# The first batch of a retention block by chunks of 128 tokens in half-array products, with other load and step orders

## Chip, cores and metric

One core of a Trainium2 chip runs the whole program. The metric is the device time of one execution in microseconds (us); lower is better. The kernel before takes 1019.66 us (median of 3 runs, 1018.57 to 1022.64).

## The reference

Retention (attention with a decay in place of the softmax) over 8 batches, 8 heads, 576 tokens and a head width of 64, then a feed-forward block over the 4608 x 512 result, all in float32:

```
scores = scale * q @ k^T                            # per batch and head, 576 x 576
Dmat   = gamma[h] ** (i - j) where i >= j, else 0
ret    = (scores * Dmat) @ v
x      = ret as (8*576) x (8*64)                    # the bridge
g      = x @ w_gate                                 # 512 x 1536
out    = (g * sigmoid(g) * (x @ w_val)) @ w_out     # 1536 x 512
```

The q, k and v are float32; the three weights come as float64.

## The kernel before

**Tiling.** Two heads make a pair, one in partitions 0 to 63, the other in 64 to 127, so a batch has four pairs (HP = 4). Pairs are numbered through all batches: 0 to 3 are the first batch, 4 is the second batch's first. The sequence is cut into chunks of L = 64 tokens; the first batch takes its first 512 tokens here (CW = 512, eight chunks) and its last 64 later, by `end_scores` and its kin. A chunk's output is the product of its own masked scores with v ("own values") plus the product of q with a running state of all earlier chunks ("earlier values").

**One pair of the first batch.** Loads of q, k, v (two heads each, 128 KB apiece). For pairs 1 to 3, q comes in another layout into `early[i]`, and GpSimd (POOL) scales it by the decay into place (`scale_run`, line 735). TensorE (PE) transposes k and q into PSUM banks (line 466); ScalarE (ACT) or VectorE (DVE) copies them to `kT` and `qT` (lines 470 to 473). k is scaled by its decay (`keys`, lines 505 and 507). Then TensorE makes the scores of the eight chunks (line 573, 64x64 products in `inner`), and each chunk's k^T v (`new_states`, line 543). DVE masks the scores with `near` (line 580) and combines the k^T v sums into states (lines 596 to 608). TensorE makes own values (line 532) and earlier values (line 559) in `outer`; DVE or ACT puts them into `xs[0]` (lines 645, 640). A float32 product is two matmul records in the trace.

**The feed-forward's first tile** is the 512 tokens of the first batch. `up0(f, chunks)` makes the hidden block f of 12: for gate and for val, four products over c = 0 to 3 (one per pair) into a bank, 128x512 each (line 853; for some f in halves, line 850). f = 0 uses bankA and bankB, f = 1 bankC and bankE. With c = 3 done, ACT takes the Silu of the gate (line 856) and DVE multiplies with val (line 857).

**Weights** are float64 in HBM and are made float32 in the kernel: `load_w(m)` loads the raw bits (`order` gives which), `split(j)` on ACT makes two parts of a half j (lines 389 and 390), `rounding(j)` on DVE joins them (lines 406 and 407) and then calls `split(j + 1)`. Halves 0 and 1 are gate and val of f = 0, 2 and 3 those of f = 1, 4 and 5 the gate of f = 2 and 3. A raw place is loaded anew once its splits are done; `held` keeps one such load for later. m < 5 goes by SyncE's queue (SP), the rest by ACT's.

**Order.** Behind `tc.manual_schedule` the order on every engine is the program's own; each engine takes its instructions in turn. Before that point a scheduler orders the first loads and selects. The first batch runs in `tick(t, 0, HP)` for t = 0 to 5, in the branch `hi == HP`: pair t is transposed, t - 1 gets scores and states, t - 2 its values. Pairs alternate between two sets of buffers (`places`). At t = 4 and 5 the first up steps stand between: up0(0, c = 0, 1), up0(1, c = 0, 1), then c = 2 and 3. `tick(HP, HP, FIRST)` begins the second batch, with up0(2) next.

Of the kernel before, what the change touches and what calls it, by code (L numbers as in the profile page):

```python
# [22 lines left out]
def tables(gamma, scale, L):  # L23
# [13 lines left out]
    runs = scale * (g[None, :, None] ** ((4 * lane[:, :, None] + np.arange(4)) % L)).reshape(2 * L, -1)  # L37
    parts = [twice((g[:, None] ** -at).T), twice((g[:, None] ** (L - at)).T),
             both(g[:, None] ** L), both(g[:, None] ** (2 * L)), pieces, runs, both(scale * g[:, None] ** at),
# [92 lines left out]
def kernel(  # L132
# [121 lines left out]
    def load(i):  # L254
# [6 lines left out]
        if i < HP:  # L261
# [4 lines left out]
            for h, queue in zip(heads, queues):  # L266
                if scaled(i):
                    queue.dma_start(out=early[i][:, ts(h % 2, CW // 2)], in_=q[b, h, 0:CW].rearrange("(p c) d -> p (c d)", c=NFULL))
                else:
                    queue.dma_start(out=blocks(qk)[:, h % 2], in_=q[b, h, 0:CW].rearrange("(c p) d -> p c d", p=P))  # L270
            for h, queue in zip(heads, queues):
                queue.dma_start(out=blocks(kn)[:, h % 2], in_=k[b, h, 0:CW].rearrange("(c p) d -> p c d", p=P))
            for h in heads:
                queues[i % 2].dma_start(out=blocks(t)[:, h % 2], in_=v[b, h, 0:CW].rearrange("(c p) d -> p c d", p=P))
# [21 lines left out]
    def chunk(i, hl, c):  # L296

        if whole(i):
            g, r = divmod(NC * hl + c, 2)
            return half[r], slice(g * D, (g + 1) * D)  # L300
        if c + 1 == NC:
            return half[hl], slice(CW, CW + D)
# [7 lines left out]
    NCOL = 6 * H + 4 * HP  # L310
    nc.sync.dma_start(out=tab[:, 0:NCOL], in_=decays[:, 0:NCOL])
    load(0)
    load(1)
    ident = const.tile([P, P], F32, name="ident")
    make_identity(nc, ident)
    nc.scalar.activation(out=io[:, 0:1], in_=ident[:, 0:1], func=AF.Silu)
    inv, key = tab[:, 0:H], tab[:, H : 2 * H]
    step = tab[:, 2 * H : 2 * H + 2 * HP]
    piece = tab[:, 2 * H + 2 * HP : 2 * H + 4 * HP]
    run = tab[:, 2 * H + 4 * HP : NCOL]  # L320
# [12 lines left out]
    for rows in half:  # L333
        decay(slice(0, H), slice(0, H), rows)

    load(2)
    nc.sync.dma_start(out=tab[:, NCOL:], in_=decays[:, NCOL:])
    load(3)
# [72 lines left out]
    for f in range(2):  # L411
        for m in range(2):
            load_w(m, (f,))
    load_w(2)
    load_w(3)

# [4 lines left out]
    other = (spare[:, 0:CW].rearrange("p (h c i) -> p h c i", h=2, i=L), None,  # L421
             spare[:, CW : CW + NC * D].rearrange("p (c d) -> p c d", d=D))
# [5 lines left out]
    for t in (state, other[2]):  # L428
        nc.gpsimd.memset(t[:, 0], 0.0)

    def places(i):
        return other if i < HP and i % 2 else (ret, ret_last, state)

# [10 lines left out]
    def vector(i):  # L444

        return i == 0

    def transposes(i):
        p = i % HP
        qk, kn, vt = loaded.pop(i)  # L450
        qT = early[i] if i < HP else qp.tile([P, S], F32, tag="qT", name="qT")
# [3 lines left out]
        copy = nc.scalar.copy if i else nc.vector.tensor_copy  # L455
        if i < HP:

            mine = (bankC, bankE) if i + 1 == HP else (bankB, bankA)
            parts = [(kT, kn, mine[0]), (qT, qk, mine[1])]
            if i == 0:  # L460
                parts.reverse()

            def turn(t, src, bank):
                for c in range(NFULL):
                    to = bank[:, c : 4 * P : NFULL] if t is qT and scaled(i) else bank[:, ts(c, P)]
                    nc.tensor.transpose(to, src[:, ts(c, P)], ident)

            def put(t, _, bank):
                if i or t is qT:
                    copy(t[:, 0:CW], bank)  # L470
                else:
                    copy(t[:, 0 : CW // 2], bank[:, 0 : CW // 2])
                    nc.scalar.copy(t[:, CW // 2 : CW], bank[:, CW // 2 :])

            if i + 1 == HP:
                for part in parts:
                    turn(*part)
                pieces = [lambda part=part: put(*part) for part in parts]
# [1087 lines left out]
```

## Time and profile before

| What | us |
|---|---|
| median of 3 runs | 1019.66 |
| profiled execution | 1019.5 |
| its span, first to last instruction | 1017.8 |
| PE busy / DVE busy / ACT busy / POOL busy in the span | 1001.0 / 715.5 / 286.4 / 555.2 |
| PE's longest wait in the first 260 us: for the first q | 4.5 |
| the next: in front of line 532, behind line 389 on ACT | 2.0 |
| the next: line 864's bankE for DVE's line 857, at 125.6 | 1.1 |

Span and busy times are of the profiled execution. Engines work side by side, so a busy share says little by itself; what counts is which engine waits for which at which place. PE is busy for 98% of the span, so time is to be had where PE waits. "L466" is line 466. In a row of the timeline, `x32` counts the records, the bracket gives the engine's idle time before and what ended it, and a matmul's end is modelled: the next one may begin before it. The first profiled instruction starts at 0.

### The profile page before, as it was taken

To read this page: it belongs to the slowest core of one execution; us is meant where nothing else is said; L and a number is where in the kernel's file an instruction comes from. 1 tells how busy PE (TensorE), PEld (TensorE's weight loads), DVE (VectorE), ACT (ScalarE), POOL (GpSimd) and SP (SyncE) were. 2 spreads that over 40 slices of the span, in tenths; PEclk is the share of its full clock that TensorE was granted. 3 is DMA by queue.
4 is the path that set the end of the run, shared out by engine and by line. 5 is a ranking of instruction groups with operands and counts; after the bars stand their busy time and mean duration, and the time that the engine had idled before them with its cause. 6 is when DMAs were issued, how large, how long until landed. Compare 5 with 4: busy or idle time off the path is not lost.

```text
span 1017.8 us, 21317 instructions
## 1 busy us (share of the span) xinstructions
PE 1001.0 (98%) x8336; PEld 823.8 (81%) x8336; DVE 715.5 (70%) x1215; ACT 286.4 (28%) x636; POOL 555.2 (55%) x579
## 2 busy tenths in 40 slices
PE   6999999999999999999999999999999999999998
PEld 4654455888888888888888888888888888888887
DVE  5478887678787765967778678866575767566644
ACT  4465622122423312133322102233320012232110
POOL 3400349979472218575565247756672586566615
PEclk9999999999999999999999999999999999999999
DMA  9999977867586887657677777434454554445552
GB/s 243 256 258 246 222 223 251 253 202 198 136 248 166 248 216 209 189 172 195 177 210 204 184 183 207 166 125 167 163 174 141 150 192 145 148 159 174 186 160 94
DMA packets 278892, 194.38 MB, mean 191 GB/s; under 512 B 212552, under 2 KB 246088, under 8 KB 278792
## 3 DMA queue, kind: packets, MB, share of 16 engines
q1 hardware_dynamic: 251464, 94.70, 36.5%
q10 hardware_dynamic: 26688, 97.92, 29.1%
q8 instruction: 66, 1.08, 0.4%
q0 software_dynamic: 640, 0.39, 0.2%
q14 instruction: 34, 0.28, 0.1%
HBM read 154.04 MB, written 38.93 MB: 190 GB/s over the span
## 4 chain that ended last, share of the span: by engine, by line
PE 85%; DMA 6%; DVE 4%; ACT 2%; POOL 2%; issue 1%; SPq 0%; ACTq 0%; DVEq 0%; POOLq 0%
PE bankB L1186 11%; PE bankC L1186 11%; PE bankA L1186 11%; PE bankE L1186 11%; PE bankB L1381 7%; PE bankC L1381 7%; PE bankE L1381 6%; PE bankA L1381 6%; PE outer L1186 2%; PE inner L1186 2%; DMA kn<-in_k_dram 2%; PE outer L532 2%; PE outer L559 1%; DMA rest<-in_moe_w_val_dram 1%; PE inner L573 1%
## 5 line engine op out<-in xcount | busy, mean ns | idle before, releaser
L1042 POOL TENSOR_TENSOR rest<-rest 128x512 f32<-128x512 f32 (+1 forms) x141 | 150.3, 1077 | 162.5 <-DVE rest L1042 114.2
L1201 POOL TENSOR_TENSOR arena<-rest,io 128x256 f32<-128x256 f32 x156 | 115.0, 749 | 75.9 <-ACT io L1200 75.3
L1200 ACT ACTIVATE io<-rest 128x256 f32<-128x256 f32 x192 | 79.3, 417 | 205.1 <-DVE rest L1042 140.8
L1186 PE MATMUL bankB<-rest,arena 128*128 128x256 f32 x448 | 114.6, 380 | 0.2 <-DVE rest L1042 0.2
L1186 PE MATMUL bankC<-rest,arena 128*128 128x256 f32 x416 | 106.5, 381 | 0.0
L1042 DVE TENSOR_TENSOR rest<-bankB,rest 128x512 f32<-128x512 f32 x116 | 78.4, 684 | 39.7 <-PE bankB L1186 26.4
L1186 PE MATMUL bankA<-rest,arena 128*128 128x256 f32 x412 | 104.7, 379 | 0.0
L1042 DVE TENSOR_TENSOR rest<-bankA,rest 128x512 f32<-128x512 f32 x110 | 74.4, 684 | 38.8 <-PE bankA L1186 19.3
L1042 DVE TENSOR_TENSOR rest<-bankC,rest 128x512 f32<-128x512 f32 x110 | 74.5, 684 | 38.7 <-PE bankC L1186 25.6
L1042 DVE TENSOR_TENSOR rest<-bankE,rest 128x512 f32<-128x512 f32 x106 | 71.6, 683 | 35.5 <-PE bankE L1186 17.0
L1186 PE MATMUL bankE<-rest,arena 128*128 128x256 f32 x372 | 95.2, 381 | 0.7 <-DVE rest L1042 0.7
L1186 PEld LDWEIGHTS bankB<-rest,arena 128*128 128x128 f32 x448 | 84.7, 190 | 12.2 <-DVE rest L1042 0.6
L1186 PEld LDWEIGHTS bankC<-rest,arena 128*128 128x128 f32 x416 | 78.4, 190 | 11.9 <-DVE rest L1042 1.2
L1186 PEld LDWEIGHTS bankA<-rest,arena 128*128 128x128 f32 x412 | 78.2, 190 | 10.7
L1186 PEld LDWEIGHTS bankE<-rest,arena 128*128 128x128 f32 x372 | 70.0, 190 | 11.8 <-DVE rest L1042 1.6
L1042 POOL TENSOR_TENSOR arena<-arena 128x256 f32<-128x256 f32 (+1 forms) x76 | 70.6, 953 | 10.5 <-DMA up<-arena 6.0
L886 POOL TENSOR_TENSOR rest<-rest 128x512 f32<-128x512 f32 x21 | 28.5, 1377 | 74.7 <-DVE rest L407 59.4
L1381 PE MATMUL bankB<-arena 128*128 128x256 f32 x264 | 61.0, 381 | 0.0
L1381 PE MATMUL bankE<-arena 128*128 128x256 f32 x264 | 60.8, 380 | 0.0
L886 POOL TENSOR_TENSOR arena<-arena 128x768 f32<-128x768 f32 x24 | 47.0, 1961 | 16.0 <-DVE arena L1201 15.4
L1381 PEld LDWEIGHTS bankE<-arena 128*128 128x128 f32 x264 | 50.0, 190 | 6.8
L1381 PEld LDWEIGHTS bankB<-arena 128*128 128x128 f32 x264 | 49.8, 190 | 6.9
(267 smaller groups left out, 1886.7 us busy)
## 6 DMA issues: line engine op xcount, KB each, us to landing
arena<-up ACTq DMA_DIRECT2D x63, 896.0 KB, 4.6
arena<-dn ACTq DMA_DIRECT2D x65, 384.0 KB, 3.0
arena<-dn SPq DMA_DIRECT2D x39, 384.0 KB, 3.2
out_dram<-rest SPq DMA_DIRECT2D x31, 256.0 KB, 3.2
qk<-in_q_dram SPq DMA_DIRECT2D x108, 72.0 KB, 4.3
qk<-in_k_dram SPq DMA_DIRECT2D x108, 72.0 KB, 3.0
dn<-rest SPq DMA_DIRECT2D x26, 256.0 KB, 2.7
up<-arena SPq DMA_DIRECT2D x13, 512.0 KB, 6.4
```

What stands on the lines that cost most here:

```text
L532: m = nc.tensor.matmul(value(i, hl, c), s["v"][rows, at], ret[rows, c % 2 if whole(i) else hl, c // 2], start=start, stop=start, skip_grou ...
L559: nc.tensor.matmul(xr[half[hl]] if c + 1 == NC else value(i, hl, c), state[half[hl], c, :], s["qT"][half[hl], ts(c, L)], start=False, stop ...
L573: nc.tensor.matmul(sc[chunk(i, hl, 2 * c + r)[0], r if whole(i) else hl, c], kT[half[hl], at], qT[half[hl], at], start=True, stop=True, sk ...
L886: eng.tensor_tensor(out=dst, in0=srcs[0], in1=srcs[1], op=ALU.add if op[0] == "add" else ALU.subtract)
L1042: eng.tensor_tensor(out=out, in0=a, in1=b, op=ALU.add if sign > 0 else ALU.subtract)
L1186: m = nc.tensor.matmul(b[:, g * TB : (g + 1) * TB], w[:, g], x, start=(opens and g == 0), stop=True, skip_group_check=True)
L1200: nc.scalar.activation(out=s, in_=src[:, 0:TB], func=AF.Silu)
L1201: (nc.vector if busy and o != 2 else nc.gpsimd).tensor_tensor(out=hid[:, qd, 2 * H + h, 2 * T + t], in0=src[:, TB : 2 * TB], in1=s, op=ALU ...
L1381: nc.tensor.matmul(b[:, m * TB : (m + 1) * TB], lhs[:, qd, ts(m, P)], w[:, qd], start=(opens and qd == 0 and m == 0), stop=(qd == NQ - 1), ...
```

## The change

Of the first batch's four pairs, and of the loads around them, it changes this:

- The first batch leaves `tick` and gets functions of its own (`first_turn`, `first_put`, `first_scores`, `first_masks`, `first_sums`, `first_states`, `first_values`, `first_out`). A chunk has 128 tokens: four chunks instead of eight. Scores are 64 rows by 128 columns of the array, 128 columns moving, 8 products per pair instead of 16; sums are 128 rows by 64 columns, 8 instead of 16; own values 128 rows by 64 columns with 128 columns moving, 8 instead of 16; earlier values 6 instead of 14.
- A mask of its own, `first_near` (128 x 8 x 128, one select of 1024 columns on POOL) in place of the first two selects of `near`, which are now made later. The masked scores are 1024 columns per pair instead of 512. Three state steps per pair instead of five DVE steps. The output of a pair is one instruction of 512 columns.
- All four pairs use the same buffers: `inner` for scores, one half of `outer` for values and the other for sums, one set for masked scores; all transposes go through bankC and bankE.
- Loads: the first table grows from 64 to 208 columns and goes behind the first q half; pair 1's q and k go ahead of the v of pairs 0 and 1; the first half of the first gate block goes ahead of pair 3, and the rest of the tables behind all first weights. Pair 4's load is called first of all in the hand-written part.
- The order: up0(0) gate, c = 0 to 2, stands ahead of the fourth pair's scores, up0(0) val ahead of its values, and up0(1) follows; `rounding(1)` stands behind the fourth pair's states, `rounding(3)` behind the steps with c = 3 of up0(0); the held load and `split(4)` stand behind up0(1).

The core of the diff; first tables and loads:

```
-    runs = scale * (g[None, :, None] ** ((4 * lane[:, :, None] + np.arange(4)) % L)).reshape(2 * L, -1)
+    runs = scale * (g[None, :, None] ** ((4 * lane[:, :, None] + np.arange(4)) % (2 * L))).reshape(2 * L, -1)
...
+                if i == 0 and queue is nc.sync:
+                    nc.sync.dma_start(out=tab[:, 0:NCOL], in_=decays[:, 0:NCOL])
...
-            for h in heads:
-                queues[i % 2].dma_start(out=blocks(t)[:, h % 2], in_=v[b, h, 0:CW].rearrange("(c p) d -> p c d", p=P))
+
+            def values():
+                for h in heads:
+                    queues[i % 2].dma_start(out=blocks(t)[:, h % 2], in_=v[b, h, 0:CW].rearrange("(c p) d -> p c d", p=P))
+
+            loaded[i] = (qk, kn, t)
+            return values
...
-    NCOL = 6 * H + 4 * HP
-    nc.sync.dma_start(out=tab[:, 0:NCOL], in_=decays[:, 0:NCOL])
-    load(0)
-    load(1)
+    NCOL = 8 * H + 4 * HP + P
+    values = [load(0), load(1)]
     ident = const.tile([P, P], F32, name="ident")
     make_identity(nc, ident)
     nc.scalar.activation(out=io[:, 0:1], in_=ident[:, 0:1], func=AF.Silu)
+    for f in values:
+        f()
+    load(2)()
...
-    for rows in half:
-        decay(slice(0, H), slice(0, H), rows)
-
-    load(2)
-    nc.sync.dma_start(out=tab[:, NCOL:], in_=decays[:, NCOL:])
-    load(3)
+    first_near = arena[:, 2048:3072].rearrange("p (h i) -> p h i", i=P)
+    first_ret = arena[:, 1024:2048].rearrange("p (h c i) -> p h c i", h=2, i=P)
+    nc.gpsimd.affine_select(out=first_near, in_=first_inv.unsqueeze(2).to_broadcast([P, H, P]), compare_op=ALU.is_ge, fill=0.0,
+                            base=0, channel_multiplier=-1, pattern=[[0, H], [1, P]])
...
-    for f in range(2):
-        for m in range(2):
-            load_w(m, (f,))
+    load_w(0, (0,))
+    load(3)()
+    load_w(1, (0,))
+    for m in range(2):
+        load_w(m, (1,))
     load_w(2)
     load_w(3)
+    nc.sync.dma_start(out=tab[:, NCOL:], in_=decays[:, NCOL:])
```

The pair's new functions:

```
+    def first_scores(i):
+        for c, hl in first:
+            nc.tensor.matmul(inner[:, hl, ts(c, P)], kT[half[hl], ts(c, P)], st[i]["qT"][half[hl], ts(c, P)],
+                             start=True, stop=True, skip_group_check=True)
+
+    def first_masks(i):
+        for hl in range(2):
+            nc.vector.tensor_tensor(out=first_ret[:, hl], in0=inner[:, hl].rearrange("p (c i) -> p c i", i=P),
+                                    in1=first_near[:, 2 * i + hl].unsqueeze(1).to_broadcast([P, NFULL, P]), op=ALU.mult)
+
+    def first_sums(i):
+        s = st[i]
+        for c, hl in first:
+            nc.tensor.matmul(sums[half[hl], c], s["kn"][:, head(c, hl)], s["v"][:, head(c, hl)],
+                             start=True, stop=True, skip_group_check=True)
+
+    def first_states(i):
+        (nc.scalar.copy if i else nc.vector.tensor_copy)(out=even[:, 0], in_=sums[:, 0])
+        for c in range(1, NFULL):
+            nc.vector.scalar_tensor_tensor(out=even[:, c] if c + 1 < NFULL else end_states[:, i], in0=even[:, c - 1],
+                                           scalar=step[:, HP + i : HP + i + 1], in1=sums[:, c], op0=ALU.mult, op1=ALU.add)
+
+    def first_values(i):
+        s = st.pop(i)
+        for c, hl in first:
+            own = nc.tensor.matmul(outer[half[hl], 0, ts(c, P)], s["v"][:, head(c, hl)], first_ret[:, hl, c],
+                                   start=(c == 0), stop=(c == 0), skip_group_check=True)
+        wait = nc.tensor.nop()
...
+        for c, hl in first[2:]:
+            nc.tensor.matmul(outer[half[hl], 0, ts(c, P)], even[half[hl], c - 1], s["qT"][half[hl], ts(c, P)],
+                             start=False, stop=True, skip_group_check=True)
+
+    def first_out(i):
+        if i:
+            nc.scalar.copy(out=xs[0][:, i], in_=outer[:, 0])
...
```

`first_turn` makes the eight transposes of a pair, `first_put` its copies and the scaling of k. The order by hand, with pairs 2 and 3 in full:

```
-    for t in range(HP + 2):
-        tick(t, 0, HP)
-
-        if t == 3:
-            load(HP)
-        for j in {3: (1,), 5: (4, 5)}.get(t, ()):
-            rounding(j)
-    for c in range(2, HP):
-        for f in range(2):
-            up0(f, [c])
+    early_chunks = range(HP - 1)
+    load(HP)
+    scale_run(1)
+    first_turn(0)
+    first_put(0)
+    first_scores(0)
+    scale_run(2)
+    first_turn(1)
+    first_masks(0)
+    first_put(1)
+    first_sums(0)
+    first_states(0)
+    first_values(0)
+    first_out(0)
+    first_scores(1)
...
+    first_scores(2)
+    first_masks(2)
+    first_sums(2)
+    first_states(2)
+    split(0)
+    first_values(2)
+    first_out(2)
+    first_turn(3)
+    first_put(3)
+    rounding(0)
+    up0(0, early_chunks, (0,))
+    first_scores(3)
+    first_masks(3)
+    first_sums(3)
+    first_states(3)
+    rounding(1)
+    up0(0, early_chunks, (1,))
+    first_values(3)
+    first_out(3)
+    rounding(2)
+    up0(1, early_chunks, (0,))
+    up0(0, [HP - 1])
+    rounding(3, False)
+    up0(1, early_chunks, (1,))
+    up0(1, [HP - 1])
+    while held:
+        held.pop()()
+    split(4)
+    for j in (4, 5):
+        rounding(j)
     load(HP + 1)
+    decay(slice(0, H), slice(0, H), half[0])
```

## The prediction

> **What bounds the kernel now.** First the page: how much of the span TensorE (PE) works, and in which slices it doesn't.
>
> ```profile
> span 1017.8 us, 21317 instructions
> PE 1001.0 (98%) x8336; PEld 823.8 (81%) x8336; DVE 715.5 (70%) x1215; ACT 286.4 (28%) x636; POOL 555.2 (55%) x579
> ...
> PE   6999999999999999999999999999999999999998
> ```
>
> TensorE idles 16.8 us in all, and the one poor slice is the first (25.4 us each). Next the windows of 10 us, to place it. The columns are busy time and number of instructions of PE, PEld, DVE, ACT, POOL, then clock, DMA share and GB/s.
>
> ```profile
> 0.00:10.00 10.00, 4.44 (x74) 3.51 (x75) 1.64 (x4) 2.23 (x4) 3.21 (x11) 1.00 0.96 202
> 10.00:20.00 10.00, 8.06 (x265) 6.67 (x264) 7.66 (x17) 3.80 (x9) 3.90 (x4) 1.00 1.14 262
> 20.00:30.00 10.00, 7.80 (x146) 4.88 (x143) 6.18 (x13) 8.07 (x17) 1.95 (x2) 1.00 1.02 288
> 30.00:40.00 10.00, 9.82 (x81) 4.71 (x80) 4.70 (x11) 5.32 (x10) 6.78 (x13) 1.00 0.99 229
> 40.00:50.00 10.00, 10.00 (x44) 8.15 (x43) 4.72 (x8) 2.68 (x5) 5.71 (x11) 1.00 1.19 275
> ```
>
> The idle time is 5.56 + 1.94 + 2.20 + 0.18 = 9.9 us before 40 us; from 40 to 260 us the same view loses 1.3, of which 1.14 lies at 120 to 130. So a change of this stage can give at most 9.9, and TensorE's lateness at 41 us is passed on nearly whole. Last the timeline of the stage (start, duration).
>
> ```profile
> 9.72 1.11 PE L466 MATMUL bankB<-ident,kn 128*128 128x128 f32 x4 [0.15 <-DMA kn<-in_k_dram]
> 14.30 0.66 PE L466 MATMUL bankB<-ident,rest 128*128 128x128 f32 x4
> 18.90 0.69 DVE L580 TENSOR_TENSOR ret<-inner,near 128x512 f32<-128x512 f32 x1 [0.35 <-ACT even L584]
> 20.12 1.13 ACT L640 COPY rest<-outer 128x256 f32<-128x256 f32 x3 [1.25 <-PE outer L559]
> 23.51 0.59 ACT L470 COPY kT<-bankC 128x512 f32<-128x512 f32 x1
> 24.60 1.98 PE L853 MATMUL bankA<-rest,arena 128*128 128x512 f32 x4
> 25.18 0.43 DVE L406 TENSOR_SCALAR arena<-rest 128x512 int32<-128x512 int32 x1 [0.72 <-ACT rest L389]
> 25.75 0.69 DVE L407 CUSTOM_DVE_ANT_0 arena<-arena,rest 128x1024 uint16<-128x1024 uint16 x1
> 28.23 0.69 PE L573 MATMUL inner<-rest,kT 64*64 64x64 f32 x32
> 28.75 0.65 PE L543 MATMUL inner<-v,rest 64*64 64x64 f32 x32
> 29.33 1.98 PE L853 MATMUL bankC<-rest,arena 128*128 128x512 f32 x4
> 30.98 1.10 DVE L603 SCALAR_TENSOR_TENSOR rest<-rest,tab 128x64 f32<-128x64 f32 x3
> 35.58 0.66 ACT L389 ACTIVATE rest<-rest 128x512 f32<-128x512 f32 x1
> 36.26 1.02 PE L853 MATMUL bankC<-rest,arena 128*128 128x512 f32 x2
> 37.12 1.02 PE L853 MATMUL bankE<-rest,arena 128*128 128x512 f32 x2
> 39.04 0.60 ACT L856 ACTIVATE io<-bankA 128x512 f32<-128x512 f32 x1 [0.47 <-PE bankA L853]
> ```
>
> From these come the prices. An up step (one c, one bank) is 0.86 (36.26 to 37.12). A full-array f32 record costs 0.43 for 512 columns, so 0.11 for 128; a product is two records. Thirty-two 64x64 records take 0.52 (28.23 to 28.75), four side by side. DVE needs 0.69 for a product on 128x512 from PSUM, 1.10 for three dependent 128x64 steps, 0.43 + 0.69 for one rounding. ACT needs 0.59 for a 128x512 copy and, by the rows of line 390 that follow line 389 by 0.57, 1.24 for one split. Before, up steps begin at 24.60 and up0(2) (line 850) at 41.41: 16.81, nearly without a gap.
>
> **The front: pairs 0 to 2.** Per pair TensorE does 16 score records, 16 for own values and 12 for earlier ones at 128 columns and 16 sums at 64, two side by side: 8 x 0.11 + 8 x 0.11 + 6 x 0.11 + 8 x 0.06 = 2.9, against 32 + 32 + 32 + 28 records at some 0.52 each, 2.1, before. No row shows half-array products; the ends are 2.1 (as the quadrants) and 5.7 (52 records one after another at 0.11 or 0.06, or each pair behind a 0.19 weight load). I take 2.9, since the nearest row, the quadrants, runs neighbours at once.
>
> The Trainium skill, TensorEngine Tiling (Array Packing), Key Properties, says that a change of tiling mode drains the array, and this change makes four or five per pair. The trace here shows less: line 853 begins at 29.33, before the modelled end of line 543 at 29.40. A drain of 0.2 at each would add an estimated 1.0 in the fourth pair.
>
> But the order in which a pair's steps follow each other decides, not their sum: scores 0.9 + 0.2 until the last has ended; masks 2 x 0.69 = 1.4 (one before: twice as many columns); states 1.1 on DVE behind the masks (own values lie under this); earlier values 0.65 + 0.2; hand-overs 0.15. That is 4.4 per pair, since the next pair's scores stand behind the earlier values. Pair 0's scores start at 7.8 (line 573 now: 7.58; the wider first table, 104 KB instead of 32, puts 0.3 ahead of k at 250 GB/s), at half rate as line 466 at 9.72 (1.11 against 0.66), so 9.8; its earlier values end at 14.3 because pair 1's transposes and its own sums come between. Pair 1 ends at 19.0, pair 2 at 23.4, the fourth pair's transposes (1.0) at 24.2. So the first up step starts at 24.2 instead of 24.60: -0.4, with -2.5 (products as the quadrants, a shorter pair 0) and +2.5 (0.8 more per pair) as ends.
>
> What goes at nothing: the new mask table on POOL (1024 columns; two selects of 512 took 1.37) is ready at 6.5 and needed at 9.8; the old masks are next used at 60.6. k of pair 1 comes about 1.8 earlier, since v is put behind; but the pair's transposes wait for pair 0's scores at 9.6 anyway. The w_gate half that rounding(0) needs comes at some 15 instead of 19.45, and isn't awaited. Fewer ACT and DVE instructions (1.13 to 0.59 per output, two state steps fewer) are in the 4.4.
>
> **The three waits behind it.** From 24.2 TensorE has the same work as before: 16 up steps x 0.86 = 13.76 and the fourth pair's 2.9 + 0.2, 16.8. But its order, and DVE's, are fixed by hand:
>
> - bankB's first three steps need rounding(1), which on DVE stands behind masks(3) and states(3). These begin when scores(3) end: 0.25 tail + 1.4 + 1.1 + 1.12 + 0.1 = 4.0, less the sums (0.5) that TensorE does meanwhile: 3.5 idle. Before, this rounding ended at 24.5.
> - bankE's steps need rounding(3), now behind the first product of line 857, which needs bankB's last step: 0.3 + 0.69 + 1.12 = 2.1 idle.
> - up0(2) needs rounding(4), and so split(4), which ACT now does after both Silus: from the end of bankE's last step 0.2 + 0.69 + 0.43 + 0.69 + 0.05 = 2.1 on DVE (ACT's side, Silu 0.6 and split 1.24 from bankC's end 0.86 earlier, takes 1.2). Idle 2.1.
>
> Together 7.7. Late next: the load of the third val weights on ACT's queue goes out after these Silus, near 46 instead of 29.60, and its gate after split(5), near 49 instead of 36.85; ACT's Silu and split queue stand behind them. They are needed by up0(4) at about 67 (60.13 now); a load like these took 6.05 (36.85 to 42.90) and 9.21, so 10 us of cover are left. On SP the big table (256 KB, 1 us) now stands ahead of pair 4's q, needed by transposes at 43.35 now, later after. ACT's load itself waits for a q load of pair 5 that SP issues behind the m=4 weights; I put its landing at 45.5 +- 1, so 0 to 1.5 more; I take 0.
>
> **The sum.** -0.4 + 7.7 = +7.3 at up0(2): 48.7 instead of 41.41. Of this 1.1 comes back, the wait of bankE L864 for DVE at 125.6, whose chain runs through loads that are no later (bounds 0 and 1.1). +6.2 on the profiled execution's 1019.5 (span 1017.8 and 1.7 around it; 0.16 under the median shown, 1019.66): **1025.7**. The ends: start -2.5 to +2.5, the ACT wait +1.5, the return 0 to 1.1; its own range is 1023.5 to 1028.5.
>
> **Rivals.**
> - *The front is much quicker* (8%). If masks and states overlap the next pair's scores, so that a pair costs scores and masks alone (2.5), the first up step is at 17.6, and 17.6 + 16.8 + 7.7 = 42.1, +0.7 - 1.1: **1019.1**, not slower. It decides from a first up step before 18.0. For it: q and k come earlier, DVE idles 8.4 of the first 10 us. Against: one mask buffer, one pair of score banks, and own values before the next scores on TensorE.
> - *The waits are half covered* (12%): **1022**, +2.4. The first mask needs half the scores only, and masks start 0.2 earlier, or bankA's steps end later than DVE's front part. Against: rounding(1) cannot pass states(3).
> - *TensorE falls back to half rate in the first wait* (8%). The rows show both rates (1.11 and 0.66), with the clock given as 1.00 in both. If 3.5 us idle bring it back, bankB's three steps cost 2.6 more: **1028.3**. Against: the 2.02 idle before 23.12 did not. The Trainium skill, TensorE: Matmul & The Clock Gate, Part 1, states this rule, with an idle window of about 3.4 us that runs freely; so 3.5 would rarely hold a whole one.
> - *The half-array products don't run side by side* (10%), so the change doesn't do what it says: 2.8 more per pair, three pairs in the front and one behind, of which some 3 lie under DVE: +8, **1034**.
>
> **Chances.** Forecast 62%. The measurement can tell 0.5% (5.1 us) from no change. Faster by that needs half of the 9.9 idle, the far end of the first rival: 3%. Within it: the rest of the first two rivals (17%) and the part of the forecast under 1024.8 (19%): 36%. Slower: the other 43% of the forecast and the last two rivals: 61%. The range that holds 8 in 10 reaches from the quick front to the half rate: 1019.0 to 1029.5.
>
> **What would show it.** Right: three TensorE gaps, about 3.5 before bankB's first step (released by rounding), 2 before bankE's, 2 before up0(2), near 28, 40 and 46 us; first up step at 24 +- 2; two masks of 0.69 per pair; TensorE without idle from 49 to 130. Wrong: a first up step before 20, or no gap over 1 us in front of bankB; score products over 1.3 long; or a new wait of TensorE for weights between 50 and 130.

## The result, and the profile after

The changed kernel takes 1033.69 us (median of 5 runs, 1032.24 to 1035.66), the kernel before beside it 1019.66 (5 runs, 1018.29 to 1022.64): ratio 1.0145, 95% interval 1.0130 to 1.0159. It is slower by 14, where 6 were predicted and 1029.5 was the end of the range.

The page of the changed kernel: span, TensorE's line, its busy share and its granted clock in 40 slices of 25.8 us.

```profile
span 1031.3 us, 20790 instructions
...
PE 1008.6 (98%) x8080; PEld 827.9 (80%) x8080; DVE 713.3 (69%) x1210; ACT 283.7 (28%) x629; POOL 555.6 (54%) x578
...
PE   5899999999999999999999999999999999999998
...
PEclk9899999999999999999999999999999999999999
```

All of the loss is in the first two slices again, and TensorE is busy for 7.6 us *more* (1008.6 against 1001.0) with fewer instructions: there is not only idle time, the work itself runs longer. The clock row has an 8; the kernel before has none, and its up0(2) starts at 41.41 (its clock row, and a row of its timeline):

```profile
PEclk9999999999999999999999999999999999999999
...
41.41 3.62 PE L850 MATMUL bankA<-rest,arena 128*128 128x256 f32 x16
```

The windows of 10 us of the changed kernel (busy time and count of PE, PEld, DVE, ACT, POOL, then clock, DMA share, GB/s) show where:

```profile
20.00:30.00 10.00, 8.13 (x100) 6.24 (x101) 3.07 (x7) 4.31 (x9) 2.41 (x4) 1.00 1.13 287
30.00:40.00 10.00, 7.34 (x43) 3.41 (x42) 4.09 (x9) 1.70 (x4) 9.24 (x18) 0.83 0.99 201
40.00:50.00 10.00, 8.02 (x42) 3.95 (x42) 1.72 (x3) 2.31 (x4) 4.07 (x8) 0.97 1.08 196
50.00:60.00 10.00, 7.99 (x24) 4.67 (x23) 4.68 (x9) 5.68 (x11) 0.00 (x0) 0.86 0.51 164
60.00:70.00 10.00, 10.00 (x41) 7.59 (x40) 6.34 (x12) 7.35 (x13) 0.00 (x0) 1.00 0.86 218
```

From 30 to 60 us TensorE idles 6.65 us, and the granted clock is 0.83, 0.97 and 0.86 there. The waits of TensorE in the changed kernel up to 280 us (us in total, times, longest):

```profile
...
PE outer L758 <- DVE rest L752: 3.0, 2, 1.7
PE bankB L856 <- DVE arena L417: 2.7, 1, 2.7
PE bankA L853 <- DVE arena L417: 2.0, 1, 2.0
PE bankE L856 <- DVE arena L417: 1.9, 1, 1.9
PE outer L758 <- ACT rest L721: 1.4, 1, 1.4
...
```

The three waits for a rounding (line 417) are the predicted ones. The two rows of line 758, own values, are not: they belong to the front. Its timeline, in order of time (start, duration; line 735 scores, 740 masks, 752 states, 758 own values, 856 up steps):

```profile
8.09 2.08 PE L735 MATMUL inner<-rest,kT 64*128 64x128 f32 x16 [0.52 <-DVE kT L717]
10.28 1.29 DVE L740 TENSOR_TENSOR arena<-inner,arena 128x512 f32<-128x512 f32 x2 [1.72 <-PE inner L735]
13.61 0.28 DVE L752 SCALAR_TENSOR_TENSOR rest<-even,tab,outer 128x64 f32<-128x64 f32 x1
13.94 1.09 PE L758 MATMUL outer<-arena,v 128*64 128x128 f32 x16 [1.28 <-DVE rest L752]
15.11 0.87 PE L764 MATMUL outer<-rest,even 64*64 64x128 f32 x12
20.06 1.09 PE L758 MATMUL outer<-arena,v 128*64 128x128 f32 x16 [1.35 <-ACT rest L721]
25.48 1.09 PE L758 MATMUL outer<-arena,v 128*64 128x128 f32 x16 [1.69 <-DVE rest L752]
...
28.37 2.74 PE L856 MATMUL bankA<-rest,arena 128*128 128x512 f32 x6
...
35.47 4.54 PE L856 MATMUL bankB<-rest,arena 128*128 128x512 f32 x6 [2.66 <-DVE arena L417]
41.91 2.84 PE L856 MATMUL bankC<-rest,arena 128*128 128x512 f32 x6
48.38 4.46 PE L856 MATMUL bankE<-rest,arena 128*128 128x512 f32 x6 [1.91 <-DVE arena L417]
56.65 3.72 PE L853 MATMUL bankA<-rest,arena 128*128 128x256 f32 x16 [2.02 <-DVE arena L417]
```

Two things are to be seen. Pair 0's masks end at 11.57, but own values, which need only these, start at 13.94, just behind the last state step (13.61 + 0.28); so in pairs 1 and 2, at 20.06 and 25.48. (The list of waits names ScalarE's line 721 for pair 1, since that copy ended last, 0.03 behind the state step. In the fourth experiment below, pair 1's own values start before that copy does, so it is not what they wait for.) The first up step is at 28.37 instead of 24.60. And the same six up-step records take 2.74 and 2.84 in bankA and bankC, but 4.54 and 4.46 in bankB and bankE, right behind two of the three waits: half rate. The granted clock (third number from the right) says the same of these two stretches:

```profile
35.80:39.20 3.40, 3.40 (x5) 1.35 (x4) 0.69 (x1) 0.00 (x0) 3.35 (x7) 0.50 1.12 243
49.50:52.80 3.30, 3.30 (x6) 1.24 (x5) 0.00 (x0) 0.00 (x0) 0.00 (x0) 0.50 0.21 37
```

up0(2) starts at 56.65 instead of 41.41, 15.24 late.

### The profile page after: what moved, and what is told of

The parts are those of the page before. It is cut to its first block, busy times and chain, and to the rows that moved or that the text cites. A ratio compares the mean times of both kernels' runs of the same rounds, so it can differ in the third digit from the quotient of the medians.

```text
span 1031.3 us, 20790 instructions
## 1 busy us (share of the span) xinstructions
PE 1008.6 (98%) x8080; PEld 827.9 (80%) x8080; DVE 713.3 (69%) x1210; ACT 283.7 (28%) x629; POOL 555.6 (54%) x578
## 4 chain that ended last, share of the span: by engine, by line
PE 70%; DVE 1%; POOL 0%; SPq 0%; DMA 0%; ACTq 0%; issue 0%; ACT 0%; DVEq 0%
PE bankC L1189 9%; PE bankB L1189 9%; PE bankA L1189 9%; PE bankE L1189 9%; PE bankB L1384 7%; PE bankE L1384 7%; PE bankC L1384 7%; PE bankA L1384 6%; PE outer L1189 2%; PE inner L1189 2%; PE outer L501 1%; PE outer L528 1%; PE inner L542 1%; PE inner L512 1%; DVE rest L1045 0%; SPq L290 0%
## 5 line engine op out<-in xcount | busy, mean ns | idle before, releaser
L1045 DVE TENSOR_TENSOR rest<-bankC,rest 128x512 f32<-128x512 f32 x110 | 74.6, 685 | 39.1 <-PE bankC L1189 25.3
L1189 PEld LDWEIGHTS bankE<-rest,arena 128*128 128x128 f32 x372 | 70.1, 190 | 11.1 <-DVE rest L1045 0.9
L889 POOL TENSOR_TENSOR arena<-arena 128x768 f32<-128x768 f32 x24 | 47.0, 1962 | 15.3 <-DVE arena L1204 14.6
```

The source lines that it names most:

```text
L889: eng.tensor_tensor(out=dst, in0=srcs[0], in1=srcs[1], op=ALU.add if op[0] == "add" else ALU.subtract)
L1045: eng.tensor_tensor(out=out, in0=a, in1=b, op=ALU.add if sign > 0 else ALU.subtract)
L1189: m = nc.tensor.matmul(b[:, g * TB : (g + 1) * TB], w[:, g], x, start=(opens and g == 0), stop=True, skip_group_check=True)
```

## The experiments

The stage is read by two times of each run's profile, which is one execution: the first up step, and up0(2)'s start. Medians are of 4 to 12 runs; the kernel before ran beside each group. "After" is the changed kernel.

| Run | first up step | up0(2) | median us | before beside it | ratio, 95% interval |
|---|---|---|---|---|---|
| before | 24.60 | 41.41 | 1019.66 | | |
| after | 28.37 | 56.65 | 1033.69 | 1019.66 | 1.0145 (1.0130 to 1.0159) |
| 1 rounding(1) early | 28.00 | 50.16 | 1028.77 | 1019.85 | 1.0099 (1.0075 to 1.0123) |
| 2 rounding(3) early | 27.93 | 52.34 | 1031.08 | 1019.85 | 1.0120 (1.0100 to 1.0141) |
| 3 split(4) early | 27.66 | 53.89 | 1031.13 | 1019.85 | 1.0120 (1.0099 to 1.0142) |
| 4 sums in another bank | 24.34 | 52.62 | 1028.65 | 1019.85 | 1.0093 (1.0074 to 1.0113) |
| 5 first wait filled | 28.14 | 53.03 | 1032.63 | 1018.86 | 1.0131 (1.0116 to 1.0147) |
| 6 second wait shifted | 28.01 | 53.15 | 1031.09 | 1018.86 | 1.0117 (1.0102 to 1.0132) |
| 7 all of 1 to 4 | 25.11 | 49.81 | 1029.79 | 1018.86 | 1.0112 (1.0095 to 1.0129) |
| 8 a load behind the Silus | 23.90 | 41.70 | 1028.61 | 1019.32 | 1.0091 (1.0075 to 1.0108) |
| 9 the same, warm start | 23.32 | 42.55 | 1028.04 | 1019.32 | 1.0080 (1.0060 to 1.0100) |
| 10 before, warm start | 24.89 | 41.70 | 1019.11 | 1019.32 | 0.9997 (0.9987 to 1.0006) |
| 11 that load behind the splits | 24.77 | 42.57 | 1024.69 | 1018.58 | 1.0068 (1.0054 to 1.0081) |
| 12 the same, warm start | 22.48 | 41.06 | 1026.88 | 1018.58 | 1.0086 (1.0066 to 1.0106) |
| 13 that load on SyncE | 24.80 | 42.60 | 1020.16 | 1020.17 | 1.0003 (0.9989 to 1.0018) |
| 14 the same, warm start | 22.29 | 40.09 | 1020.70 | 1020.17 | 1.0002 (0.9987 to 1.0017) |
| 15 before, late load | 24.19 | 41.39 | 1018.87 | 1020.17 | 0.9983 (0.9968 to 0.9998) |

### 1 to 3: each wait by itself

The first moves rounding(1) up on VectorE, the second rounding(3), the third split(4) and rounding(4):

```
     rounding(0)
+    rounding(1)
     up0(0, early_chunks, (0,))
...
     first_states(3)
-    rounding(1)
```

```
     up0(1, early_chunks, (0,))
+    rounding(3, False)
     up0(0, [HP - 1])
-    rounding(3, False)
```

```
     rounding(3, False)
+    while held:
+        held.pop()()
+    split(4)
+    rounding(4)
     up0(1, early_chunks, (1,))
     up0(1, [HP - 1])
-    while held:
-        held.pop()()
-    split(4)
-    for j in (4, 5):
-        rounding(j)
+    rounding(5)
```

> The changed kernel with rounding(1) on VectorE moved from behind the fourth pair's states to right behind rounding(0). Theory (the waits of the hand-written order, and half rate behind them, are most of the loss): the wait of 2.66 us ahead of bankB's first up step goes, its six records take 2.7 instead of 4.54, so up0(2) starts at 52.1 instead of 56.65 and the time is 4.5 lower, about 1029. Rival A (the lateness comes from loads, and a wait removed here turns into a wait for weights or states later): up0(2) is moved by less than 1 and the time stays within 1 of 1033.7. Rival B (the half rate has another cause than the wait, such as the traffic of that stretch): the wait goes but the six records still take about 4.5; time 2.7 lower, 1031.

> The changed kernel with rounding(3) put ahead of the steps with c = 3 of up0(0), so that on VectorE it stands in front of the product of line 860. Theory: the wait of 1.91 ahead of bankE's first step goes and its six records take 2.7 instead of 4.46, so up0(2) starts at 53.0 and the time is 3.7 lower, about 1030. Rival A: no gain, within 1 of 1033.7. Rival B: 1.9 lower, 1031.8, with the records still at 4.5.

> The changed kernel with the held load, split(4) and rounding(4) put right behind rounding(3), ahead of the rest of up0(1). Theory: the wait of 2.02 ahead of up0(2) goes, up0(2) starts at 54.6 instead of 56.65, time 2.0 lower, about 1031.7; the loads of the third val and gate weights go out some 7 us earlier and this changes nothing more. Rival A (the later loads are what costs): the gain is clearly above 2, 3 to 6 us, since the loads come earlier. Rival C (the wait only moves to the next rounding or to Silu): within 0.7 of 1033.7.

Each wait goes with its edit and nothing takes its place, so rivals A and C fall; B falls too, since the records behind a wait that is gone run at full rate (2.84 and 2.74 for six). The half rate does something that no theory had said. The timeline of the first experiment:

```profile
32.37 2.84 PE L856 MATMUL bankB<-rest,arena 128*128 128x512 f32 x6
...
43.58 2.84 PE L856 MATMUL bankE<-rest,arena 128*128 128x512 f32 x6 [1.91 <-DVE arena L417]
...
50.16 3.72 PE L853 MATMUL bankA<-rest,arena 128*128 128x256 f32 x16 [2.02 <-DVE arena L417]
```

The wait ahead of bankE is as long as it was, 1.91, but the half rate behind it is gone too: up0(2) is 6.5 earlier instead of 4.5 (0.4 of it since the front began earlier), the time 4.9 lower. The timeline of the second experiment has it the other way round:

```profile
45.87 2.74 PE L856 MATMUL bankE<-rest,arena 128*128 128x512 f32 x6
...
52.34 5.41 PE L853 MATMUL bankA<-rest,arena 128*128 128x256 f32 x16 [2.02 <-DVE arena L417]
```

Here the last wait, 2.02 as before, is followed by 5.41 for records that took 3.72: the half rate has moved there, and the time is 2.6 lower instead of 3.7. So the length of a wait does not decide. What does is read from the records: where the rate changes inside a row. In the changed kernel the half rate ends at 39.23 and again at 52.88 (from the steps from record to record: 0.43 at full, 0.85 at half rate), 13.65 apart, and each stretch is 3.4 long, so 13.65 is four times 3.41. With borders every 3.41 us from there, each wait falls so (2, 3 and 4 have half-rate stretches of their own to take the borders from, the first only the end of its slow start, near 11.5):

| Run | wait | idle in one window of 3.41 | rate in the next window |
|---|---|---|---|
| after | 32.81 to 35.47 | 2.66 | half |
| after | 46.47 to 48.38 | 1.91 | half |
| after | 54.63 to 56.65 | 1.67 and 0.35 | full |
| 1 | 41.67 to 43.58 | 0.55 and 1.36 | full |
| 1 | 48.14 to 50.16 | 0.91 and 1.11 | full |
| 2 | 50.33 to 52.34 | 2.02 | half |
| 3 | 45.89 to 47.80 | 1.91 | half |
| 4 | 42.44 to 44.35 | 1.91 | half |
| 4 | 50.60 to 52.62 | 1.75 and 0.27 | full |

A window with 1.91 us or more of idle time halves the next one; with 1.75 it doesn't. The Trainium skill, TensorE: Matmul & The Clock Gate, Part 1, has the window (3413 ns, free-running), and the borders here agree with it. The Trainium skill, in the same part, has the clock fall after at least one idle window of about 3.4 us. Read as a window that is idle throughout, this differs from the measurement: a little over half a window is enough.

### 4: why own values waited

```
-    sums = outer[:, 1, 0 : NFULL * D].rearrange("p (c d) -> p c d", d=D)
+    sums_of = lambda i: (outer[:, 1, 0 : NFULL * D] if i + 1 == HP else (bankA, bankB)[i % 2][:, 0 : NFULL * D]).rearrange("p (c d) -> p c d", d=D)
...
```

> The changed kernel with the k^T v sums of pairs 0 to 2 in bankA and bankB (free until the first up step) instead of in the second half of the tile that also takes the values. Nothing is left out. Theory (own values wait for the states only because sums and values share a tile, and this is what makes a pair's cycle 6 instead of 4.4 us): own values start at the end of the masks, the first up step at 24.5 +- 0.7 instead of 28.37, all behind it unchanged, time 3.9 lower, about 1029.8. Rival D (the loads of k and q set the front's pace): the own values start earlier but the next transposes or scores wait for loads, first up step not before 27.5, time within 1 of 1033.7.

The timeline of this kernel (its lines are one further down):

```profile
12.17 1.04 PE L759 MATMUL outer<-arena,v 128*64 128x128 f32 x16
...
16.81 1.05 PE L759 MATMUL outer<-arena,v 128*64 128x128 f32 x16
...
24.34 2.74 PE L857 MATMUL bankA<-rest,arena 128*128 128x512 f32 x6
```

Own values start without a wait over 0.3 us, and the first up step is at 24.34: 4.0 earlier, as expected. The median is 5.0 lower where 3.9 were expected; the profiled execution (1029.82) is the longest of the four. In the built program the first own-values product of the changed kernel waits for the count that VectorE reaches behind the states; with the sums in another bank it waits for the masks' count. Sums and values share one tile, `outer`, in two halves; that the sharing makes own values wait for the states' reading is shown, by which rule the wait is set is not. Rival D falls.

### 5 and 6: the half rate by itself

The fifth fills the first wait with three products whose result is overwritten; the sixth adds 1.28 us of such work to the first experiment's kernel, ahead of bankB's steps, which shifts the second wait and leaves its length.

```
     first_sums(3)
+    for c in early_chunks:
+        nc.tensor.matmul(bankE, w_up[:, 0, 0, 0, c // 2, (c % 2) * P : (c % 2 + 1) * P], xs[0][:, c, :], start=True, stop=True)
```

```
     first_sums(3)
+    for at in (slice(0, 512), slice(0, 256)):
+        nc.tensor.matmul(bankE[:, at], w_up[:, 0, 0, 0, 0, 0:P], xs[0][:, 0, at], start=True, stop=True)
```

> The changed kernel with three products of 512 columns (0.86 each) into bankE, whose result is overwritten and not used, put on TensorE behind the fourth pair's sums, so that the wait of 2.66 ahead of bankB's first step is filled with work; bankB still starts when rounding(1) is done. Theory (the half rate comes from TensorE's idleness in windows of 3.41 us that run through without regard to the program: a window with 1.9 idle or more halves the next one, one with 1.66 does not): bankB's six records take 2.8 instead of 4.54; that moves the wait ahead of bankE by 1.7, it then lies across a border of two windows (1.3 and 0.6 idle), so bankE's six take 2.8 as well; up0(2) at 53.3 instead of 56.65 and the time 3.4 lower, 1030.3. Rival A (any wait of about 2 us halves the rate behind it): bankB at 2.8, bankE still at 4.5, up0(2) at 55.0, 1032. Rival B (the half rate is due to the traffic or to the other engines in that stretch): no change, bankB at 4.5, 1033.7.

> The kernel with rounding(1) early (first experiment) and one product of 512 and one of 256 columns more, 1.28 us, with an unused result, ahead of bankB's first step. Nothing else is changed; the wait ahead of bankE keeps its length of 1.91 but starts 1.28 later, at about 43.0, so that it lies inside one window (42.2 to 45.6) instead of across the border at 42.2. Theory (fixed windows): TensorE falls to half rate behind it for one window, bankE's and the next steps cost 1.7 more, up0(2) at 53.1 instead of 50.16 and the time 3.0 higher than the first experiment's, 1031.7, although only 1.28 of work was added. Rival (the rate depends on the length of the wait or on what ran before it): up0(2) at 51.4, 1.3 higher, 1030.1.

The timeline of the fifth, and then of the sixth:

```profile
35.25 2.84 PE L856 MATMUL bankB<-rest,arena 128*128 128x512 f32 x6
...
46.46 2.84 PE L856 MATMUL bankE<-rest,arena 128*128 128x512 f32 x6 [1.91 <-DVE arena L417]
...
53.03 3.72 PE L853 MATMUL bankA<-rest,arena 128*128 128x256 f32 x16 [2.01 <-DVE arena L417]
```

```profile
33.78 2.74 PE L856 MATMUL bankB<-rest,arena 128*128 128x512 f32 x6
...
44.88 4.54 PE L856 MATMUL bankE<-rest,arena 128*128 128x512 f32 x6 [1.91 <-DVE arena L417]
...
53.15 3.72 PE L853 MATMUL bankA<-rest,arena 128*128 128x256 f32 x16 [2.02 <-DVE arena L417]
```

Both profiles are as the windows said, to 0.3 us: in the fifth, work of no use in the first wait takes the half rate away from both places; in the sixth, 1.28 us of work cost 2.99 at up0(2) (53.15 against 50.16), because the same wait of 1.91 now lies inside one window. The medians follow less closely: the fifth's is 1032.63, not 1030.3, with runs from 1030.37 (the profiled one) to 1033.29, and the sixth's 1031.09 instead of 1031.7. The fifth's median is nearer to the 1032 of its rival A, whose mechanism its profile rules out. The borders lie at another place in each execution (the slow start ended between 11.1 and 11.9 in these profiles), so that a run can fall on the other side. The granted clock of every execution fits this in the fifth: 1.000 in the run of 1030.37, 0.998 in the three of 1032.60 to 1033.29, and 1.7 us lost of 1031 is 0.0017. In the sixth it doesn't order the runs (1.000 at the longest, 1031.74), so that this alone makes the spread is not shown.

### 7 to 9: all four together, and a fifth cost

The seventh joins the four edits, with one step moved further than in the third: split(4) and rounding(4) stand ahead of up0(0)'s last steps, and so ahead of both Silus on ScalarE.

```
     up0(1, early_chunks, (0,))
-    up0(0, [HP - 1])
     rounding(3, False)
...
     split(4)
...
+    rounding(4)
+    up0(0, [HP - 1])
+    up0(1, early_chunks, (1,))
...
```

> The changed kernel with all four edits: rounding(1), rounding(3) and split(4) with rounding(4) early, and the sums of pairs 0 to 2 in a bank of their own. Theory: first up step at 24.3, no wait of TensorE over 0.5 from there to up0(2), no half rate behind the start; up0(2) at 24.3 + 18.2 (first experiment's 50.16 - 28.00 less its waits of 1.91 and 2.02) = 42.5, where the kernel before has 41.41; time 1.1 over the kernel before, 1020.8, same within 0.5%. Rival 1 (the half-array products were worth something that the waits hid): up0(2) before 41.4 and a time under the kernel before. Rival 2 (the later loads or the wider tables cost on their own): a new wait for weights or loads between 30 and 130, 1023 or more.

The theory failed: 1029.79. Rival 2 had the time and the kind of wait. The front and the up steps go through without a wait up to 43.1, and then up0(2) waits for 6.74. TensorE's row and ScalarE's queue in the timeline of the seventh:

```profile
48.73 0.38 ACTq L380 DMA_DIRECT2D rest<-in_moe_w_gate_dram  x1
49.16 0.60 ACT L860 ACTIVATE io<-bankA 128x512 f32<-128x512 f32 x1 [10.02 <-DMA rest<-in_moe_w_gate_dram]
49.81 5.89 PE L854 MATMUL bankA<-rest,arena 128*128 128x256 f32 x16 [6.74 <-ACT io L860]
```

Silu(0) (line 860) could have run at 39.1, but ahead of it on ScalarE's queue stands the issue of a load: rounding(4) calls split(5), and split(5) issues the load m = 6. In the built program this issue waits until an earlier transfer with the same semaphore, m = 4 (issued at 35.64), has landed. It went out at 48.73; ScalarE stood still for 10.02. The eighth experiment puts rounding(4) behind the first Silu, and split(5) with this load behind the second:

```
     split(4)
-    rounding(4)
     up0(0, [HP - 1])
+    rounding(4, False)
     up0(1, early_chunks, (1,))
     up0(1, [HP - 1])
+    split(5)
     rounding(5)
```

The ninth adds, in TensorE's empty start, products on a cleared buffer:

```
+    nc.vector.memset(xs[0][:, 0], 0.0)
+    def keep_busy(n):
+        for _ in range(n):
+            nc.tensor.matmul(bankA[:, 0:P], xs[0][:, 0, 0:P], xs[0][:, 0, 0:P], start=True, stop=True)
...
+    keep_busy(7)
...
```

> The last kernel (all four edits) took 6.7 us in front of up0(2), because split(5)'s load of the next gate weights stood on ScalarE's queue ahead of both Silus and waited there until 48.7. Here rounding(4) no longer calls split(5); split(5) with that load stands behind the second Silu. Theory (that wait was this one queue order and nothing else): Silu(0) at 38.5 and Silu(1) at 43, no wait of TensorE over 0.5 between 25 and up0(2), which starts at 42.6; time 1.1 over the kernel before, about 1020.5, same within 0.5%. Rival (the changed load order itself starves the stage): a wait for split(6), the third weights or their rounding takes its place between 42 and 60, and the time is above 1023.

> The same kernel with products of 128 columns on a cleared buffer, result unused, in TensorE's empty time at the start: seven ahead of the first transposes, two ahead of k's, one ahead of the first scores. Theory (the first work runs at half rate because TensorE was idle in the window before): full rate from about 5 instead of 11.5; k's transposes 0.5, the scores of pair 0 0.9 and pair 1's transposes 0.9 shorter, less up to 0.6 where loads of pair 1 are not there yet: first up step 1.7 +- 0.6 earlier, time 1.7 lower than without, about 1019. Rival (the front then waits for loads or for VectorE): first up step less than 0.5 earlier, no gain.

In the eighth, up0(2) starts at 41.70 without a wait, as the theory has it. But its val half waits for a rounding until 51.50, with half rate behind it:

```profile
51.50 5.56 PE L854 MATMUL bankB<-rest,arena 128*128 128x256 f32 x16 [6.18 <-DVE arena L417]
```

This rounding needs split(6), which is now queued behind the same load, issued at 49.02. So the rival had the place and the time. The ninth gained 0.6 at the first up step, where 1.7 were expected, and lost it to the same load.

### 10 to 15: the load order

The eleventh issues that load behind rounding(7), the thirteenth goes back to the seventh's order and sends it by SyncE's queue; the twelfth and fourteenth are these with the warm start; the tenth and fifteenth put the warm start, and the late load, into the kernel before.

```
-            if j == 3:
+            if j in (3, 5):
                 held.append(lambda: load_w(m + RAWS + (m < RAWS)))
...
+    plan.append(lambda: held.pop()())
```

```
-        i, queue = order[m], nc.sync if m < 5 else nc.scalar
+        i, queue = order[m], nc.sync if m < 5 or m == 6 else nc.scalar
```

> The kernel before with the same products in its empty start (seven, one, one) and nothing else changed. Theory: scores and sums of pair 0 at full rate, but pair 1's transposes wait for k until 9.57 as before and then take 1.26 instead of 2.17; first up step 0.9 earlier than 24.60 and 0.9 lower than the kernel before. Rival: the wait of 2.02 at 21.1 to 23.1 in that kernel takes it up, no gain.

> As the eighth experiment, but the load of the next gate weights (the one that ScalarE's queue held until 49.0 because an earlier transfer had not landed) is issued only behind rounding(7), so that split(6), split(7) and split(8) are not queued behind it. Theory (the floor of about 50 us under up0(2)'s second half is this one issue in front of the splits): up0(2) at 41.7, its val half at 45.2, up0(3) at 48.6 without a wait over 0.5; time within 0.3% of the kernel before, about 1020. Rival (the transfers themselves, 1 MB that needs 13 us from issue to landing, set the floor): a wait of several us for split(8) or the third val weights at 52 to 60, time above 1024.

> The same with the products in TensorE's empty start (seven, two, one). Theory: first up step 0.6 earlier than without (as between the eighth and ninth experiment, 23.90 and 23.32), time 0.5 lower, about 1019.5, not to be told from the kernel before. Rival: a wait for loads takes it back, no difference to the run without.

> The kernel with all four edits (seventh experiment, split(5) early) and one change more: the load of the next gate weights, m = 6, goes out by SyncE's queue, ahead of the fifth pair's loads, instead of by ScalarE's. Theory (behind the four waits there is a fifth cost, the order of the loads: m = 5 and m = 6 go out late, or block ScalarE until an earlier transfer lands): ScalarE is not held up, m = 6 goes out at 39 to 44, nothing of TensorE waits over 0.5 up to 110; up0(2) at 42.5 and the time 0.5 to 1.5 over the kernel before, about 1020, with a spread of its runs like the kernel before's (3 us). Rival (the transfers' bandwidth in that stretch is the bound, whatever the queue): waits of 2 to 4 us for weights between 50 and 110, 1023 to 1027.

> The same with the products in TensorE's empty start (seven, two, one). Theory: first up step 0.6 to 2 earlier than without, time 0.5 lower than without, 1019.5, not to be told from the kernel before. Rival: no difference to the run without, since loads take it up.

> The kernel before with one edit: the load m = 6 is issued only behind rounding(7), at about 47 instead of 36.85. Theory (a late m = 6 is by itself a cost, once TensorE is at up0(2) by 42): waits of TensorE for ScalarE's Silu or for roundings between 55 and 110, time 2 to 6 us above the kernel before, 1021 to 1025, with a wide spread. Rival (10 us of cover are there, as the prediction took): no change, within 0.5 of the kernel before.

The thirteenth goes as its theory said. Its timeline, then its windows:

```profile
24.80 2.74 PE L857 MATMUL bankA<-rest,arena 128*128 128x512 f32 x6
...
42.60 3.62 PE L854 MATMUL bankA<-rest,arena 128*128 128x256 f32 x16
46.05 3.62 PE L854 MATMUL bankB<-rest,arena 128*128 128x256 f32 x16
```

```profile
30.00:40.00 10.00, 9.93 (x47) 4.82 (x46) 4.79 (x10) 4.58 (x8) 8.97 (x17) 1.00 1.03 200
40.00:50.00 10.00, 10.00 (x42) 7.66 (x41) 5.16 (x10) 4.74 (x9) 1.50 (x3) 1.00 1.09 307
50.00:60.00 10.00, 10.00 (x97) 6.18 (x96) 7.15 (x15) 6.57 (x12) 0.00 (x0) 1.00 0.94 221
```

No wait over 0.15 us from the first up step to 100, clock 1.00, ratio 1.0003 (0.9989 to 1.0018): with these five edits the whole loss of 14 is gone. The fifth edit changes two things at once, the queue of the load and its time (issued at 38.68 instead of 48.73). The fifteenth parts them, and its theory failed: in the kernel before, the same load at 49.91 instead of 36.85 costs nothing. So the lateness of the transfer by itself is no cost there; in the seventh and eighth it is what stands behind the issue on ScalarE's queue that waits.

The eleventh has the late load too. Its profiled run is as its theory said (span 1019.7), yet its median is 1024.69 with runs from 1021.43 to 1027.16, and the twelfth's profile has waits of 3.6 and 2.7 for Silus, between 60 and 140, behind loads on ScalarE's queue. Why that order swings so much stays open. The warm start makes the first up step up to 2.5 earlier (22.29 against 24.80) and gives nothing clear of the noise in any pair of runs, so the theories of the tenth and twelfth failed: in the fourteenth TensorE idles 4.06 us between 100 and 130, in the thirteenth 2.16, in the kernel before 1.14. In the tenth, loads and GpSimd's scaling of k take it up before the first up step. No version of the changed kernel beats the kernel before.

## Why the prediction was wrong

**The stage, and what passes on: right.** All of the loss is ahead of up0(2); of its 15.2 us 13.5 are left in the span, so 1.7 came back, 1.1 were taken. The predicted wait-free stretch from up0(2) to 130 is there.

**The front: wrong by 4.2 (28.37, not 24.2).** The step that failed is "own values lie under this", in the cycle of 4.4 per pair. The mechanism was taken from the data that own values need; the built program made them wait for the states. In the trace a cycle is 6.1 (scores at 15.91 and 22.01), and 1.15 of it are own values, which come behind the states instead of under them. The fourth experiment gives the bank and gets 24.34. That this is so near to 24.2 is in part luck. The recorded terms of the cycle add up to 4.6, not 4.4, and 23.4 and 1.0 make 24.4. And there the cycle of 4.6 (scores at 14.18 and 18.82) is not the chain through masks and states that was added up, but TensorE's own work: it idles 0.8 of the 16.4 us from the first scores to the first up step, with dearer products (below) and the states under them.

**The products: side by side, but mis-sized.** Scores, own values, earlier values and sums take 1.09, 1.15, 0.80 and 0.6 by their starts, 3.6 per pair, where 2.9 was taken and the kernel before needs 2.1 by the prediction's row. (The 52 records of its upper end are 60; that end, two times 2.9, hardly moves.) Two records side by side do take 0.11 within a group, as taken; 0.2 to 0.3 more come once per group, at the change from one shape of product to the next. Behind own values the program also waits for the last of them, so there the change alone is not shown. The Trainium skill, TensorEngine Tiling (Array Packing), Key Properties, says that a change of tiling mode drains the array; the trace agrees with it. The prediction had estimated 1.0 for this in the fourth pair and set it aside; the four groups cost 0.7 per pair more than taken. Behind the front, 28.37 to 56.65 less waits and half rate is 18.3, where 16.8 was taken, 1.5 more; in the thirteenth experiment, without the waits, the same stretch is 17.8 (24.80 to 42.60), so about 1.0 of this is dearer work and 0.5 goes with the three stops. That the repaired kernel ends at parity and not below it fits this, but no run shows it alone.

**The three waits: right in place, cause and nearly in size**, 2.66, 1.91 and 2.02 against 3.5, 2.1 and 2.1. Experiments 1 to 3 took away each one.

**The half rate: the rival at 8% happened, twice.** The step that failed is the argument against it, "the 2.02 idle before 23.12 did not", with the thought that a wait must fill a whole window. It must fill a little over half of one, and where it lies decides. Each stretch cost 1.7, so 3.4 in all, where the rival had 2.6 once.

**The loads: right that they are covered, wrong in what is queued behind them.** "10 us of cover are left" holds for the transfer (the fifteenth experiment). But the prediction named ScalarE's Silu and splits as what stands behind these loads and costed the landing alone; the seventh and eighth show that an issue can hold that queue for 6 to 10 us. In the changed kernel these loads go out behind both Silus (53.87 and 56.73), and nothing waits for them up to 130.

Together at up0(2): front 3.8 later than before, waits 6.6, half rate 3.4, work behind the front 1.5, which is 15.3 where 15.24 were measured. Against the predicted 7.3 that is 4.2 more in the front, 1.1 less in the waits, 3.4 and 1.5 more.

## What to carry to other kernels

Read what an instruction waits for from the built program, not from the data it needs: two halves of one tile can be tied together, and a free bank is then worth more than a shorter product. Cost a wait of TensorE with what may follow it: here over half a window idle made the next 3.4 us run at half rate, a loss of 1.7, and filling the wait with useless work is a cheap test of that. Before repairing the waits of one stage, ask what they hide; here a load's issue on ScalarE's queue took their place until it was moved to a queue with nothing urgent behind it.

## What the runs showed of the hardware

TensorE's rate is set window by window: 3.41 us long, at places that the program doesn't set; 1.91 us idle in one halve the next, 1.75 don't (nine waits above). At half rate less is enough to keep it there: in the twelfth experiment a half-rate window (118.6 to 122.0) with 1.1 us idle was followed by another, at a granted clock of 0.50 in both. Of the waits of 1.91 to 2.02 us in the changed kernel and the first six experiments, five were followed by half rate and seven by full rate, with the same instructions around them.

ScalarE stood idle for 10.0 and 6.7 us (seventh and eighth experiment) behind the issue of a transfer on its queue, which in the built program waits until another transfer has landed (in the seventh one of 1 MB, issued 13 us before by another engine); the activations behind it waited too.
